# Attention and two MLPs on one core: product banks and sum banks of the second MLP as tiles of their own, weight sums moved to GpSimd, loads and stores issued a step later

## The chip, the cores and the metric

The kernel runs on one core of one Trainium2 chip. The metric is device time in microseconds (us) of one execution; shown are the median of three runs and one further execution that was profiled. Engines go by the profile's names: PE is the matrix engine, PEld its weight load, DVE, ACT and POOL are VectorE, ScalarE and GpSimd, and SP is the queue that issues all the DMAs spoken of here.

## The reference

```python
attn = softmax(q @ k.T / 8 + bias(pos))            # 4 batches, 8 heads, 576 positions, 64 wide
x = (attn @ v).transpose(0, 2, 1, 3).reshape(2304, 512)
h = x @ w_in                                       # 512 -> 2048
x = (h - tanh(h)) @ w_out                          # 2048 -> 512
g = sigmoid(x @ w_gate) * (x @ w_val)              # 512 -> 1536, twice
return g @ w_out2                                  # 1536 -> 512
```

Weights come as 64-bit floats in memory and are turned into pairs of 32-bit parts on the chip. A matrix product in full precision is three matmuls: high by high, high by low and low by high.

## The kernel before

**Three stages.** Attention fills the first 318 us or so, the first MLP runs to about 772 us, and the second MLP from there to the end. The first MLP goes in 48 steps (`n` in the loop at L943): `first(n)` is 24 matmuls of 128x384 at L639, `fifth(m)` 24 matmuls at L703, and between them ACT, DVE and POOL compute h - tanh(h) on the step before (L656 to L684). `x_load` (L623) fetches the tokens of a coming block (tile xm), which ACT then splits (L629) and POOL (L630).

**Weights of the second MLP** are converted alongside. A raw load (`load`, L500 and L504, tile wraw) is followed by an Abs on ACT (L521), four DVE operations (L548, L549, L550, L546), a cast on ACT (L584, high part) and a subtraction on POOL (L578, low part), then a store to a DRAM scratch (L582, tile wsc). For the seven-product scheme below, sums of the four quarters of a weight block are wanted too: items c0 and c1 of `make`, four DVE operations (L536, L537, L540, L541) for each of six weight groups fp. `run` hands out all of this, step by step; the last DVE operation of an item itself calls `load`, and the POOL operation itself issues the store. Four groups are converted during the first MLP, at n = 24, 30, 36 and 42; groups 4 and 5 are converted by `convert`, two operations or fewer to a slot, in the second MLP.

**Second MLP.** It is a row of 252 slots: 3 pairs of token blocks, 6 groups fp, and 14 products in each (7 for the gate with m = 0, then 7 for the value with m = 1; a seven-product scheme takes the place of eight block products). `slot2(s)` does `product(s)`: six matmuls of 128x384 at L829 into `banks[s % 2]`; then `down()`: three matmuls of 128x512 at L845 into one of six `sums`, for the group before; then `evacuate(s)`: one DVE or ACT operation that reads the bank (L873 to L890). In 12 of the 14 slots there is a `down()`; slots 12 and 13 of each group have none (called dry here, the others wet). `posts` runs what was put off: sigmoid, product of gate and value (POOL L901), split into gh (ACT L677) and gl (POOL L864).

Where products and sums live is decided at two places. Both banks are halves of one tile of the pool `up`, and two of the six sums are halves of another:

```python
b = up.tile([128, 2, 512], F32, name="up")
banks = [b[:, i, 0:TB] for i in range(2)]
...
b = up.tile([128, 2, 512], F32, name="up")
sums = [b[:, i] for i in range(2)]
```

Waits between engines are placed per tile by the tile framework: a write to one half of a tile counts as a write to the tile.

**Reloads.** `feed()` (L783, tile w from wsc) brings converted weights back, nine transfers of 512 KB for a group, through a ring of 13 slots, as soon as a slot's last reader has been given out (`spent`).

Of the kernel before, what the change touches and what calls it, by code (L numbers as in the profile page):

```python
# [7 lines left out]
F32 = mybir.dt.float32  # L8
# [5 lines left out]
PSUM = bass.MemoryType.PSUM  # L14
# [419 lines left out]
N1 = len(STEPS)  # L434
# [8 lines left out]
X0_AT = N1 - 4  # L443
# [10 lines left out]
class Weights:  # L454


    def __init__(self, nc, wi, wo, wg, wv, wo2, stage, wsc):
        self.nc, self.stage, self.wsc = nc, stage, wsc
        col = lambda w, n, f, k0, nk: dram_ap(w.bitcast(I32), 256 * f + 256 * n * k0, [[2 * n, 128], [256 * n, nk], [1, 256]])
        row = lambda w, f: dram_ap(w.bitcast(I32), 128 * f * 2 * DM, [[2 * DM, 128], [1, 2 * DM]])  # L460
        self.of = {}
        use = [("i", f) for f in range(FA)] + [("o", f) for f in range(FA)]
        for f in range(FA, NF1):
            use += [("i", f), ("o", f)]
        self.items = []
        for i, (k, f) in enumerate(use):
            self.of[k, f] = i
            self.items.append((k, f, [row(wo, f)] if k == "o" else [col(wi, DF1, f, 0, 4)]))
        for fp in range(NFP):
            for n in range(2):  # L470
                for k in range(2):
                    self.items.append((f"u{n}{k}", fp, [col(w, DF2, 2 * fp + n, 2 * k, 2) for w in (wg, wv)]))
            self.items += [("c0", fp, None), ("c1", fp, None)]
            self.items += [("p", 2 * fp + j, [row(wo2, 2 * fp + j)]) for j in range(2)]
        self.raws = [i for i, x in enumerate(self.items) if x[2]]
        self.n = len(self.items)
        self.raw, self.tmp, self.out, self.pools, self.u = {}, {}, {}, {}, {}
        self.loaded = self.scanned = self.made = self.done = self.usable = self.staged = 0
        self.stages = STAGE1
        self.turns = -1  # L480
        self.stored = set()

    def open(self, pool, lo, hi):
        self.limit = hi
# [41 lines left out]
    def make(self):  # L526
        i = self.made
        if i >= self.scanned:
            return []
        self.made += 1  # L530
        V = self.nc.vector
        k, f, src = self.items[i]
        if k == "c0":
            self.u["s"] = self.fresh(i)
            u = dict(self.u)
            return [lambda: V.tensor_add(u["s"], u["u10"], u["u11"]),  # L536
                    lambda: V.tensor_sub(u["u10"], u["u00"], u["u10"])]  # L537
        if k == "c1":
            u = dict(self.u)
            return [lambda: V.tensor_sub(u["u11"], u["s"], u["u00"]),  # L540
                    lambda: V.tensor_sub(u["u01"], u["u01"], u["u11"])]  # L541
        r, u = self.raw.pop(i), self.tmp[i]
        hi, lo, ui = r[:, :, 1], r[:, :, 0], u.bitcast(I32)

        def last():
            V.scalar_tensor_tensor(ui, lo, 29, ui, ALU.logical_shift_right, ALU.bitwise_or)  # L546
            self.load()
        return [lambda: V.tensor_scalar(u, u, HI_MIN, HI_MAX, ALU.max, ALU.min),  # L548
                lambda: V.tensor_scalar(ui, ui, 3, 0x3FFFFFF8, ALU.logical_shift_left, ALU.bitwise_and),  # L549
                lambda: V.scalar_tensor_tensor(ui, hi, -0x40000000, ui, ALU.bitwise_and, ALU.bitwise_or),  # L550
                last]

    def split(self):
        i = self.done
        if i >= self.made:
            return [], []
        self.done += 1
        k, f, src = self.items[i]
        if k in "io":
            parts = [(None, self.tmp.pop(i))]  # L560
        elif k == "p":
            parts = [((f // 2, GROUPS2 + f % 2), self.tmp.pop(i))]
        else:
            self.tmp.pop(i, None)
            u = self.u
            parts = {"u00": [(1, u.get("u00"))], "u01": [(2, u.get("u01"))], "u10": [], "u11": [(4, u.get("u11"))],
                     "c0": [(5, u.get("s")), (7, u.get("u10"))], "c1": [(6, u.get("u11")), (3, u.get("u01"))]}[k]
            parts = [((f, PRODUCTS.index(j)), x) for j, x in parts]
        highs, lows = [], []
        for at, x in parts:  # L570
            if at is None:
                w = self.out[i] = self.slot(i)
            else:
                w = self.slot(self.stages[self.staged % len(self.stages)])
                self.staged += 1

            def low(at=at, x=x, w=w):
                self.nc.gpsimd.tensor_sub(w[:, 1], x, w[:, 0].bitcast(F32))  # L578
                if at is None:
                    self.usable += 1  # L580
                else:
                    self.nc.sync.dma_start(self.wsc[at[0]][at[1]], w.bitcast(F32).rearrange("p a c -> p (a c)"))  # L582
                    self.stored.add(at)
            highs.append(lambda x=x, w=w: self.nc.scalar.copy(w[:, 0], x))  # L584
            lows.append(low)
        return highs, lows

    def trickle(self):
        while self.done < self.limit:
# [21 lines left out]
def mlps(tc, st, xr, x0, W, xs, x2s, out, consts):  # L611


    nc = tc.nc
    V, A, G, T = nc.vector, nc.scalar, nc.gpsimd, nc.tensor
    nq, nz, warm = consts
    TB = TBS[1]
# [120 lines left out]
    pk, ps, ob = (st.enter_context(tc.tile_pool(name=n, bufs=k)) for n, k in (("p2k", 2), ("p2s", 3), ("p2o", 4)))  # L738
    only1 = ExitStack()
    pm, pq = (only1.enter_context(tc.tile_pool(name=n, bufs=k)) for n, k in (("p2m", 2), ("p2q", 1)))  # L740
    up = st.enter_context(tc.tile_pool(name="ps_u", bufs=2, space=PSUM))

    TP = 2 * TB
    sx, xw, tt_ = {}, {}, {}
# [29 lines left out]
    ring, held, issued, spent = [], {}, [0], set()  # L774

    def feed():
        while issued[0] < len(loads):
            k = issued[0]
            tau, fp, i = loads[k]
            if (fp, i) not in W.stored or k >= len(ring) and (k < RING_SLOTS or loads[k - RING_SLOTS] not in spent):  # L780
                return
            w = W.slot(ring[k % RING_SLOTS])
            nc.sync.dma_start(w.bitcast(F32).rearrange("p a c -> p (a c)"), W.wsc[fp][i])  # L783
            held[loads[k]] = w
            issued[0] += 1
# [28 lines left out]
    def mat(s):  # L814
        g, j = divmod(s, GROUPS2)
        u, m = divmod(g, 2)
        tau, fp = divmod(u, NFP)
        return tau, fp, m, j

    def product(s):  # L820
        tau, fp, m, j = mat(s)
        w = held[tau, fp, j]
        p = banks[s % 2]
        fresh = j in (0, 1, 4)
        for kp in range(2):
            x = xw[PRODUCTS[j], kp]
            for i, (a, c) in enumerate(P3):
                o = 256 * m + 128 * kp
                T.matmul(p, w[:, a, o:o + 128], x[:, c], start=(fresh and kp == 0 and i == 0),  # L829
                         stop=(kp == 1 and i == 2), skip_group_check=True)  # L830
        if m:
            spent.add((tau, fp, j))
# [80 lines left out]

    def slot2(s):
        tau, fp, m, j = mat(s)
        product(s)
        left = down()
        evacuate(s)
        if left:
            at(s + 1, left)  # L920
        for f in posts.pop(s, []):
            f()
        if tau + 1 < NPAIR:
            if fp == 1 and m == 0 and j < 4:
                src_load(tau + 1, j)
            if fp == 2 and j < 3:
                combine(m, j)
            if fp == NFP - 1 and m == 1:
                x_next(j)
        feed()  # L930

    def x_next(j):
        k = PRODUCTS[j]
# [8 lines left out]
    temps = [0]  # L942
    s = 0  # L943
    for n in range(N1 + 3):
        if n == 2:
            acc = st.enter_context(tc.tile_pool(name="ps_a", bufs=4, space=PSUM))
        acts = second(n - 1) if ok(n - 1) else []
        acts[2:2] = [lambda m=m: fourth(m) for m in due(n, 1)]
        vecs = [f for m in due(n, 0) for f in third(m)]
# [27 lines left out]
        if ok(n):  # L977
            for _ in first(n):
                if n < 2:
                    yield  # L980
        elif n == N1:
            only1.close()
            ev = st.enter_context(tc.tile_pool(name="p3e", bufs=6))
            b = up.tile([128, 2, 512], F32, name="up")
            banks = [b[:, i, 0:TB] for i in range(2)]
            W.stages = RING[RING_SLOTS:]
            for _ in range(3):
                slot2(s)
                s += 1
        elif n == N1 + 1:  # L990
            b = up.tile([128, 2, 512], F32, name="up")
            sums = [b[:, i] for i in range(2)]
            for _ in range(4):
                slot2(s)
                s += 1
# [24 lines left out]
                    combine(kp, 3)  # L1020
                x_make(j, kp, V if j in (6, 7, 3) else G)
        if n >= X0_AT:
            ring += [i for i in RING if freed[i] == n + 1]
            ring[RING_SLOTS:] = []
            feed()
        yield
# [131 lines left out]
```

## Time and profile before

| what | value |
|---|---|
| median of three runs | 1308.53 us (1308.18 to 1310.28) |
| profiled execution, its time | 1310.77 us |
| its span, first to last instruction | 1309.0 us |
| mean granted clock of PE | 0.973 |
| PE busy | 1190.9 us, 91% of the span |
| DVE, ACT, POOL busy | 63%, 51%, 46% |

The profiled execution takes 2.24 us more than the median, and 1.77 us of its time lie outside its span. Busy shares are means over stages of different kinds. Matmuls are pipelined: the duration of one is longer than the distance from one to the next, so in a stretch without gaps PE's pace is read from how many matmuls it holds. A bracket behind a row of the timeline, as [0.65 <-DVE e L890], is idle time ahead of it and what ended that.

### The profile page before, as it was taken

The page shows a single profiled execution, that of the slowest core. Times are in us where ns is not written, and L with a number is a line of the kernel's source. Part 1 is how long each engine was busy: PE and PEld are TensorE (multiplying, and loading weights), DVE is VectorE, ACT ScalarE, POOL GpSimd, SP SyncE. Part 2 cuts the span into 40 slices and gives each one's busy share as a digit, 9 for nine tenths or more (in the row PEclk, how much of TensorE's full clock was granted, in tenths as well). Part 3 has the DMA queues.
Part 4 walks back from the last instruction along what each step waited for, and adds up shares of the span by engine and source line. Part 5 has one row for each costly group of instructions (what it writes and reads, how often), then busy time and mean ns, then how long its engine had stood idle before and what let it go on. Part 6 is the DMA issues. An engine that isn't in the chain of part 4 may idle for free.

```text
span 1309.0 us, 19878 instructions
## 1 busy us (share of the span) xinstructions
PE 1190.9 (91%) x6968; PEld 975.6 (75%) x6968; DVE 830.2 (63%) x1431; ACT 661.1 (51%) x1313; POOL 605.3 (46%) x558
## 2 busy tenths in 40 slices
PE   5789999999999999888977977888999999999998
PEld 2256676666899999788977976666777777777776
DVE  8978888885798888888879764764242322422222
ACT  7978788876566776655655542332141121321111
POOL 1067777775355555654546333544242322422322
PEclk9899999999999999898988979989999999999999
DMA  6656363632133334545464646867446554353551
GB/s 215 230 165 193 112 198 116 209 102 71 39 113 113 113 113 145 209 167 184 165 217 150 236 177 221 315 252 295 164 155 232 188 204 187 145 193 146 202 197 51
DMA packets 103027, 225.65 MB, mean 172 GB/s; under 512 B 12176, under 2 KB 52368, under 8 KB 102928
## 3 DMA queue, kind: packets, MB, share of 16 engines
q1 hardware_dynamic: 102928, 224.38, 48.9%
q8 instruction: 56, 0.92, 0.3%
q14 instruction: 43, 0.35, 0.1%
HBM read 166.26 MB, written 58.08 MB: 171 GB/s over the span
## 4 chain that ended last, share of the span: by engine, by line
PE 70%; DVE 11%; ACT 6%; DMA 5%; POOL 3%; issue 3%; SPq 0%; DVEq 0%; ACTq 0%; POOLq 0%
PE up L829 20%; PE acc L703 12%; PE up L639 12%; PE acc L845 6%; PE sc L227 5%; PE pv L319 5%; PE pt L269 5%; PE up L845 2%; DMA bsc<-e 1%; POOL gl L864 1%; DVE e L876 1%; DVE e L890 1%; PE bt L75 1%; DMA xm<-xs 1%; PE pv L316 1%
## 5 line engine op out<-in xcount | busy, mean ns | idle before, releaser
L829 PE MATMUL up<-w,w 128*128 128x384 f32 x1512 | 336.3, 358 | 45.1 <-DVE e L890 22.1
L829 PEld LDWEIGHTS up<-w,w 128*128 128x128 f32 x1512 | 255.3, 190 | 139.5 <-DVE e L890 46.5
L703 PE MATMUL acc<-gh,w 128*128 128x384 f32 x768 | 205.3, 349 | 32.7 <-DVE o L719 21.9
L639 PE MATMUL up<-xt,w 128*128 128x384 f32 x1152 | 210.1, 336 | 3.8 <-DVE t L673 3.8
L639 PEld LDWEIGHTS up<-xt,w 128*128 128x128 f32 x1152 | 201.6, 189 | 6.6 <-issue 6.6
L684 POOL TENSOR_TENSOR gl<-t,gh 128x384 fp32r<-128x384 f32 x96 | 106.7, 1129 | 147.2 <-ACT gh L677 55.7
L703 PEld LDWEIGHTS acc<-gh,w 128*128 128x128 f32 x768 | 145.9, 198 | 35.8 <-issue 22.8
L259 POOL TENSOR_SCALAR n<-n,rec 128x576 f32<-128x576 f32 x144 | 121.3, 857 | 81.6 <-DVE rec L254 42.7
L864 POOL TENSOR_TENSOR gl<-e,gh 128x384 fp32r<-128x384 f32 x54 | 56.8, 1053 | 220.3 <-ACT gh L677 219.1
L578 POOL TENSOR_TENSOR w<-wu,w 128x512 fp32r<-128x512 f32 x86 | 123.0, 1435 | 61.1 <-ACT w L584 60.8
L703 PE MATMUL acc<-gl,w 128*128 128x384 f32 x384 | 133.0, 346 | 0.0
L241 DVE CUSTOM_DVE_ANT_0 n<-sc,bias 128x576 f32<-128x576 f32 x144 | 103.7, 752 | 30.5 <-PE sc L227 22.8
L248 ACT ACTIVATE n<-n,mn 128x576 f32<-128x576 f32 x144 | 111.5, 784 | 8.0 <-DVE mn L241 7.7
L890 DVE TENSOR_TENSOR e<-up,e 128x384 f32<-128x384 f32 x72 | 40.2, 558 | 90.5 <-PE up L829 90.4
L677 ACT CAST gh<-t 128x384 fp32r<-128x384 f32 x114 | 57.1, 515 | 79.4 <-POOL t L901 59.5
L845 PE MATMUL acc<-w,gh 128*128 128x512 f32 x288 | 90.9, 396 | 0.0
L669 DVE TENSOR_TENSOR t<-up,t 128x768 f32<-128x768 f32 x48 | 45.9, 956 | 65.6 <-ACT t L656 65.6
L668 ACT ACTIVATE z<-z,c 128x768 f32<-128x768 f32 x48 | 45.1, 940 | 80.6 <-DVE up L667 80.6
L269 PE MATMUL pt<-ident,n 128*128 128x128 f32 x576 | 80.2, 280 | 1.4 <-ACT at L299 1.3
L630 POOL TENSOR_TENSOR xt<-xm,xt 128x384 fp32r<-128x384 f32 x48 | 50.3, 1069 | 65.6 <-ACT xt L629 60.6
L876 DVE TENSOR_TENSOR e<-up,e 128x384 f32<-128x384 f32 x36 | 20.0, 556 | 95.0 <-PE up L829 46.0
L319 PE MATMUL pv<-at,vs 128*64 128x320 f32 (+1 forms) x512 | 79.3, 421 | 0.0
(106 smaller groups left out, 2110.5 us busy)
## 6 DMA issues: line engine op xcount, KB each, us to landing
w<-wsc SPq DMA_DIRECT2D x162, 512.0 KB, 7.2
wsc<-w SPq DMA_DIRECT2D x54, 512.0 KB, 3.9
wraw<-in_wo SPq DMA_DIRECT2D x28, 512.0 KB, 4.0
bsc<-e SPq DMA_DIRECT2D x36, 295.5 KB, 3.2
xm<-xs SPq DMA_DIRECT2D x48, 192.0 KB, 3.8
x2s<-o SPq DMA_DIRECT2D x48, 192.0 KB, 3.3
wraw<-in_wi SPq DMA_DIRECT2D x16, 512.0 KB, 4.2
wraw<-in_wg SPq DMA_DIRECT2D x24, 256.0 KB, 2.9
```

Of the source, the lines that this page charges most:

```text
L241: V.tensor_tensor_reduce(n.rearrange("p (a b) -> p a b", a=2), s[:, :, 0:288], bias[t].rearrange("p (a b) -> p a b", a=2), -0.125, 3.0e38, ...
L248: A.activation(n, n, AF.Exp, bias=m, scale=-1.0, accum_out=nsum[u, t // 4][:, t % 4:t % 4 + 1])
L259: G.tensor_scalar(n, n, nrec[u, t // 4][:, t % 4:t % 4 + 1], 1.0, ALU.mult, ALU.mult)
L269: T.transpose(pt[:, i], n[:, o:o + 128], ident)
L319: T.matmul(p[0][64 * a:64 * a + 64, 0:N], v[:, c - 1, a], main[:, c - 1, a * N:a * N + N], start=False, stop=(c == 4))
L578: self.nc.gpsimd.tensor_sub(w[:, 1], x, w[:, 0].bitcast(F32))
L639: T.matmul(p[:, 0:TB], w[:, a, 128 * kt:128 * kt + 128], x[:, c], start=(kt == 0 and i == 0), stop=(kt == 3 and i == 2))
L684: G.tensor_sub(l, x[:, j], h.bitcast(F32))
L703: T.matmul(ac[blk][d][:, 0:TB], w[:, a, 128 * d:128 * d + 128], c, start=(begin and j == 0 and i == 0), stop=(end and j == NPR - 1 and i = ...
L829: T.matmul(p, w[:, a, o:o + 128], x[:, c], start=(fresh and kp == 0 and i == 0), stop=(kp == 1 and i == 2), skip_group_check=True)
L845: T.matmul(sums[3 * t + d], g[:, c], w[:, a], start=(begin and i == 0), stop=(end and i == 2))
L864: G.tensor_sub(l, x, h.bitcast(F32))
```

## The change

Five edits. (1) The two banks and two of the sums become four tiles `sum0` to `sum3` in a pool `ps_w`, opened where the pool `up` is closed; the pool `acc` of the other sums is put on the other side of the memory so that `up` can close. (2) The weight sums c0 and c1 run on GpSimd during the first MLP and on DVE again in the second. (3) Raw loads and stores of converted parts are no longer issued by the operation that frees or fills the buffer, but through a list `pending`, one step later in the first MLP and two slots later in the second. (4) `feed()` moves from the end of a slot to its start. (5) Ring slots are opened one step later.

```diff
+        self.mix = nc.gpsimd
+        self.clock = self.lag = 0
+        self.pending = []
+
+    def later(self, f):
+        if self.lag:
+            self.pending.append((self.clock + self.lag, f))
+        else:
+            f()
+
+    def tick(self):
+        self.clock += 1
+        while self.pending and self.pending[0][0] <= self.clock:
+            self.pending.pop(0)[1]()
...
-            return [lambda: V.tensor_add(u["s"], u["u10"], u["u11"]),
-                    lambda: V.tensor_sub(u["u10"], u["u00"], u["u10"])]
+            u, M = dict(self.u), self.mix
+            return [lambda: M.tensor_add(u["s"], u["u10"], u["u11"]),
+                    lambda: M.tensor_sub(u["u10"], u["u00"], u["u10"])]
...
-            self.load()
+            self.later(self.load)
...
-                    self.nc.sync.dma_start(self.wsc[at[0]][at[1]], w.bitcast(F32).rearrange("p a c -> p (a c)"))
-                    self.stored.add(at)
+                    self.later(lambda: self.store(at, w))
...
+    W.lag = 1
...
     def slot2(s):
         tau, fp, m, j = mat(s)
+        W.tick()
+        feed()
         product(s)
...
-        feed()
...
     for n in range(N1 + 3):
+        if n < N1:
+            W.tick()
         if n == 2:
-            acc = st.enter_context(tc.tile_pool(name="ps_a", bufs=4, space=PSUM))
+            acc = st.enter_context(tc.tile_pool(name="ps_a", bufs=4, space=PSUM, side="right"))
...
-            b = up.tile([128, 2, 512], F32, name="up")
-            banks = [b[:, i, 0:TB] for i in range(2)]
+            upst.close()
+            one = st.enter_context(tc.tile_pool(name="ps_w", bufs=1, space=PSUM))
+            four = [one.tile([128, 512], F32, name=f"sum{i}") for i in range(4)]
+            banks = [x[:, 0:TB] for x in four[:2]]
             W.stages = RING[RING_SLOTS:]
+            W.mix, W.lag = V, 2
...
-            b = up.tile([128, 2, 512], F32, name="up")
-            sums = [b[:, i] for i in range(2)]
+            sums = four[2:]
...
-            ring += [i for i in RING if freed[i] == n + 1]
+            ring += [i for i in RING if freed[i] == n or n == X0_AT and freed[i] < n]
```

The first place is PE's row in the second MLP, where one group of weights ends and the next begins. Before, both banks and a sum carry the name up; the number behind it tells the tile, and 9079 is the one tile of both banks.

```order
L829 MATMUL up_9079<-w10_8851,w30_10186 128x384 x3
L829 MATMUL up_9079<-w11_8962,w30_10186 128x384 x3
L829 MATMUL up_9079<-w12_8854,w25_10188 128x384 x3
L829 MATMUL up_9079<-w13_8965,w25_10188 128x384 x3
L829 MATMUL up_9079<-w0_10314,w20_10202 128x384 x3
L829 MATMUL up_9079<-w1_10317,w20_10202 128x384 x3
L845 MATMUL up_9146<-w16_10190,gh_10368 128x512 x2
L845 MATMUL up_9146<-w16_10190,gl_10369 128x512
```

Of the change, the same place:

```order
L848 MATMUL sum0_9075<-w10_8847,w30_10192 128x384 x3
L848 MATMUL sum0_9075<-w11_8958,w30_10192 128x384 x3
L848 MATMUL sum1_9076<-w12_8850,w25_10194 128x384 x3
L848 MATMUL sum1_9076<-w13_8961,w25_10194 128x384 x3
L848 MATMUL sum0_9075<-w0_10320,w20_10208 128x384 x3
L848 MATMUL sum0_9075<-w1_10323,w20_10208 128x384 x3
L864 MATMUL sum2_9077<-w16_10196,gh_10374 128x512 x2
L864 MATMUL sum2_9077<-w16_10196,gl_10375 128x512
```

No matmul has moved; products now go by turns to two tiles, and a product waits for the evacuation two slots back in place of that one slot back.

The second place is POOL's row in the first MLP, at the step of the first sums (n = 24). gl is the low part of h - tanh(h) that PE waits for, w the low part of a weight, wu a weight on its way. Before:

```order
L684 TENSOR_TENSOR gl_6777<-t_6694,gh_6776 128x384
L684 TENSOR_TENSOR gl_6781<-t_6694,gh_6780 128x384
L578 TENSOR_TENSOR w2_6772<-wu_6686,w2_6772 128x512
L578 TENSOR_TENSOR w3_6796<-wu_6773,w3_6796 128x512
L578 TENSOR_TENSOR w0_6797<-wu_6579,w0_6797 128x512
L578 TENSOR_TENSOR w1_6808<-wu_6686,w1_6808 128x512
L578 TENSOR_TENSOR w2_6809<-wu_6493,w2_6809 128x512
L684 TENSOR_TENSOR gl_6885<-t_6769,gh_6884 128x384
```

Of the change:

```order
L701 TENSOR_TENSOR gl_6777<-t_6694,gh_6776 128x384
L701 TENSOR_TENSOR gl_6781<-t_6694,gh_6780 128x384
L550 TENSOR_TENSOR wu_6773<-wu_6575,wu_6683 128x512
L551 TENSOR_TENSOR wu_6575<-wu_6409,wu_6575 128x512
L592 TENSOR_TENSOR w2_6772<-wu_6683,w2_6772 128x512
L554 TENSOR_TENSOR wu_6683<-wu_6773,wu_6409 128x512
L555 TENSOR_TENSOR wu_6490<-wu_6490,wu_6683 128x512
L592 TENSOR_TENSOR w3_6795<-wu_6773,w3_6795 128x512
L592 TENSOR_TENSOR w0_6796<-wu_6575,w0_6796 128x512
L592 TENSOR_TENSOR w1_6805<-wu_6683,w1_6805 128x512
L592 TENSOR_TENSOR w2_6806<-wu_6490,w2_6806 128x512
L701 TENSOR_TENSOR gl_6885<-t_6769,gh_6884 128x384
```

Four sums now stand on POOL between two steps' gl, where there were five subtractions; DVE's row is the same as before without them.

The third place is SP's row at the same step. xm is the load of tokens that the next steps need. Before:

```order
L723 DMA x2s<-o 128x384 x4
L582 DMA wsc_2_66<-w_6594 128x1024
L504 DMA wraw<-in_wo 128x1024
L582 DMA wsc_5_69<-w_6772 128x1024
L582 DMA wsc_4_68<-w_6796 128x1024
L582 DMA wsc_3_67<-w_6797 128x1024
L500 DMA wraw<-in_wg 128x2x256
L500 DMA wraw<-in_wv 128x2x256
L582 DMA wsc_1_65<-w_6808 128x1024
L582 DMA wsc_6_70<-w_6809 128x1024
L623 DMA xm<-xs 128x384 x2
```

Of the change:

```order
L740 DMA x2s<-o 128x384 x4
L518 DMA wraw<-in_wo 128x1024
L602 DMA wsc_2_66<-w_6594 128x1024
L518 DMA wraw<-in_wo 128x1024
L640 DMA xm<-xs 128x384 x2
L602 DMA wsc_5_69<-w_6772 128x1024
L602 DMA wsc_4_68<-w_6795 128x1024
L602 DMA wsc_3_67<-w_6796 128x1024
L514 DMA wraw<-in_wg 128x2x256
L514 DMA wraw<-in_wv 128x2x256
L602 DMA wsc_1_65<-w_6805 128x1024
L602 DMA wsc_6_70<-w_6806 128x1024
```

The pair of xm loads that stood behind five stores and two raw loads now stands ahead of them.

## Rows read from the trace of the kernel before

**Rows 1.** Page, the chain of work that ended last, by line.

```profile
PE up L829 20%; PE acc L703 12%; PE up L639 12%; PE acc L845 6%; PE sc L227 5%; PE pv L319 5%; PE pt L269 5%; PE up L845 2%; DMA bsc<-e 1%; POOL gl L864 1%; DVE e L876 1%; DVE e L890 1%; PE bt L75 1%; DMA xm<-xs 1%; PE pv L316 1%
```

**Rows 2.** Page, costliest groups of instructions, second MLP's products and evacuation.

```profile
L829 PE MATMUL up<-w,w 128*128 128x384 f32 x1512 | 336.3, 358 | 45.1 <-DVE e L890 22.1
...
L890 DVE TENSOR_TENSOR e<-up,e 128x384 f32<-128x384 f32 x72 | 40.2, 558 | 90.5 <-PE up L829 90.4
```

**Rows 3.** Timeline of PE, wet slots, then dry ones (start, us, engine, line).

```profile
1000.10 1.32 PE L829 MATMUL up<-w,w 128*128 128x384 f32 x6
1001.26 0.63 PE L845 MATMUL acc<-w,gh 128*128 128x512 f32 x2
1001.72 0.40 PE L845 MATMUL acc<-w,gl 128*128 128x512 f32 x1
1002.07 1.32 PE L829 MATMUL up<-w,w 128*128 128x384 f32 x6
...
1015.99 1.32 PE L829 MATMUL up<-w,w 128*128 128x384 f32 x6 [0.65 <-DVE e L890]
1017.96 0.45 PE L829 MATMUL up<-w,w 128*128 128x384 f32 x1 [0.65 <-DVE e L890]
```

**Rows 4.** Timeline of DVE in the first of those slots.

```profile
1001.46 0.56 DVE L890 TENSOR_TENSOR e<-up,e 128x384 f32<-128x384 f32 x1 [1.41 <-PE up L829]
```

**Rows 5.** Windows of the core, busy time of each engine, clock and DMA.

```profile
350.00:500.00 150.00, 150.00 (x864) 149.36 (x863) 134.43 (x174) 105.77 (x172) 82.02 (x71) 1.00 0.34 109
800.00:900.00 100.00, 84.06 (x376) 65.86 (x375) 63.51 (x96) 31.82 (x62) 49.88 (x40) 0.97 0.81 298
935.00:1296.00 361.00, 341.06 (x1556) 265.10 (x1555) 99.29 (x170) 81.42 (x166) 106.09 (x104) 1.00 0.46 177
```

**Rows 6.** Timeline of PE after the last product: sums back to back.

```profile
1296.86 0.62 PE L845 MATMUL up<-w,gh 128*128 128x512 f32 x2
...
1297.55 0.62 PE L845 MATMUL acc<-w,gh 128*128 128x512 f32 x2
```

**Rows 7.** Timeline: evacuations of slots 0, 70 and 251, the last.

```profile
777.32 0.48 ACT L873 COPY e<-up 128x384 f32<-128x384 f32 x1 [1.23 <-DVE t L673]
...
935.35 0.48 ACT L873 COPY e<-up 128x384 f32<-128x384 f32 x1 [3.80 <-PE up L829]
...
1296.35 0.56 DVE L890 TENSOR_TENSOR e<-up,e 128x384 f32<-128x384 f32 x1 [1.42 <-PE up L829]
```

**Rows 8.** Timeline, a stall in the first token pair.

```profile
852.42 0.66 ACT L521 ACTIVATE wu<-wraw 128x512 f32<-128x512 f32 x1 [4.46 <-DMA wraw<-in_wv]
...
854.52 0.69 PE L829 MATMUL up<-w,w 128*128 128x384 f32 x1 [4.48 <-DVE t L886]
```

**Rows 9.** DMA issues and SP's timeline: reloads (us to landing; then us issuing).

```profile
w<-wsc SPq DMA_DIRECT2D x162, 512.0 KB, 7.2
...
1014.07 4.95 SPq L783 DMA_DIRECT2D w<-wsc  x9
```

**Rows 10.** PE's waits from 490 to 775 us (total, times, longest).

```profile
PE acc L703 <- DVE o L719: 21.9, 3, 9.0
PE acc L703 <- ACT t L656: 5.1, 1, 5.1
PE acc L703 <- ACT o L722: 4.7, 1, 4.7
```

**Rows 11.** Timelines of SP and ACT, a late load of tokens.

```profile
535.14 2.21 SPq L623 DMA_DIRECT2D xm<-xs  x2
...
541.08 1.08 ACT L629 CAST xt<-xm 128x384 fp32r<-128x384 f32 x2 [3.08 <-DMA xm<-xs]
```

**Rows 12.** Timeline of DVE, weight sums (first, last of four); page, POOL's weight subtraction.

```profile
519.96 1.19 DVE L536 TENSOR_TENSOR wu<-wu 128x512 f32<-128x512 f32 x1
...
526.98 1.67 DVE L541 TENSOR_TENSOR wu<-wu 128x512 f32<-128x512 f32 x1
...
L578 POOL TENSOR_TENSOR w<-wu,w 128x512 fp32r<-128x512 f32 x86 | 123.0, 1435 | 61.1 <-ACT w L584 60.8
```

More of the change, by code (lines that the diff above doesn't have):

```diff
@@ L534, in make @@
             self.u["s"] = self.fresh(i)
-            u = dict(self.u)
-            return [lambda: V.tensor_add(u["s"], u["u10"], u["u11"]),
-                    lambda: V.tensor_sub(u["u10"], u["u00"], u["u10"])]
+            u, M = dict(self.u), self.mix
+            return [lambda: M.tensor_add(u["s"], u["u10"], u["u11"]),
+                    lambda: M.tensor_sub(u["u10"], u["u00"], u["u10"])]
         if k == "c1":
-            u = dict(self.u)
-            return [lambda: V.tensor_sub(u["u11"], u["s"], u["u00"]),
-                    lambda: V.tensor_sub(u["u01"], u["u01"], u["u11"])]
+            u, M = dict(self.u), self.mix
+            return [lambda: M.tensor_sub(u["u11"], u["s"], u["u00"]),
+                    lambda: M.tensor_sub(u["u01"], u["u01"], u["u11"])]
         r, u = self.raw.pop(i), self.tmp[i]
@@ L586, in split, with store @@
         return highs, lows
+    def store(self, at, w):
+        self.nc.sync.dma_start(self.wsc[at[0]][at[1]], w.bitcast(F32).rearrange("p a c -> p (a c)"))
+        self.stored.add(at)
     def trickle(self):
@@ L740, in mlps @@
     pm, pq = (only1.enter_context(tc.tile_pool(name=n, bufs=k)) for n, k in (("p2m", 2), ("p2q", 1)))
-    up = st.enter_context(tc.tile_pool(name="ps_u", bufs=2, space=PSUM))
+    upst = ExitStack()
+    up = upst.enter_context(tc.tile_pool(name="ps_u", bufs=2, space=PSUM))
+    W.lag = 1
     TP = 2 * TB
```

## The prediction

> **What bounds the kernel now.** I read the page's chain first. The largest line on it is the products of the second MLP, L829, with 20% of the span [rows 1]; PE is what the kernel waits for, and the question is at which pace it could go. The group of L829 tells of only 45.1 us of idle time before its matmuls, half of it put down to DVE's evacuation L890, while L890 in turn sat idle 90.4 us waiting for L829 [rows 2]. Two engines that wait for each other by turns are a ring: product, evacuation, product. The timeline shows it. A product starts at 1000.10, its six matmuls end at 1001.42, DVE reads the bank from 1001.46 to 1002.02, and the next product starts at 1002.07 [rows 3, 4]. A wet slot is so 1.97 us. A dry slot, which has three matmuls fewer, takes 1.97 us as well (1015.99 to 1017.96), with 0.65 us idle put down to L890 [rows 3]: the slot's length is that of the ring and not of PE's work. That the next product waits for the evacuation just before it, although it writes the other bank, is because both banks are one tile.
>
> PE's busy share hides this: from 935 to 1296 it is 341 of 361 us [rows 5], because the duration of a matmul overlaps that of the next. The pace without gaps is in the first MLP: 864 matmuls of 128x384 in 150.00 us at clock 1.00, with PE busy throughout [rows 5], 0.1736 us each. Six of them are 1.04 us. Three matmuls of 128x512 take 1297.55 - 1296.86 = 0.69 us when they follow each other [rows 6].
>
> **Own tiles for the banks (edit 1).** Without the ring a wet slot is 1.04 + 0.69 = 1.73 us and a dry one 1.04 us; a group of 14 slots is 14 x 1.04 + 12 x 0.69 = 22.9 us. I add 0.2 us a group for waits that are still there (semaphores, the copies out of the sums): 23.1 us, or 1.65 us a slot. Does the evacuation keep up? A product now waits for the evacuation two slots back. In a dry slot this is the tightest: the evacuation takes 0.56 us [rows 4], and from its end there is 0.05 us to the start of the next product; the product between takes 1.04 us, so the bank is free 0.4 us early. DVE, ACT and POOL are busy 99, 81 and 106 of 361 us [rows 5], so none of them is near a bound at 300 us.
>
> From the evacuation of slot 70 (935.35) to that of slot 251 (1296.35) are 361.0 us in 181 slots, 1.994 each [rows 7]. At 1.65 they take 298.7: **-62 us**. Bounds: with no added wait (22.9) -65; with 0.05 us more in every slot -53.
>
> The reloads must keep this pace. They come as a burst of nine per group, 4.95 us to issue at slot 12, landing a median 7.2 us after issue [rows 9]; the DMA engines are busy a share of 0.46 in that stretch [rows 5], which becomes 0.46 x 361 / 299 = 0.56. The median transfer lands 7.2 us after its issue, so the nine are in some 12 us (4.95 + 7.2) after the burst's start, and the group that reads them lasts 23. Closest are the first ones: by the ring's order they are read two dry and two wet slots after the start, 2 x 1.04 + 2 x 1.73 = 5.5 us at the new pace, 7.9 now. The early ones of a burst land before the median, so I cost this at nothing, and with it edit 4, which moves `feed()` from a slot's end to the next slot's start, the same instant for SP but for what that slot itself has spent. If the cover is gone, each of the 13 groups waits 1 to 2 us, 13 to 26 in all.
>
> **The first token pair, groups 0 to 4.** From 777.32 to 935.35 its 70 slots take 158.0 us [rows 7], 2.26 each; at the steady 1.994 they would take 139.6, so 18.4 us are stalls of other kinds. One is at 847 to 855: ACT's Abs waited 4.46 us for a raw load, DVE stood behind it, and PE waited 4.48 us for DVE's evacuation [rows 8]. If all these stalls stay, the gain is that of the ring alone, 70 x (1.994 - 1.65) = 24 us. I take 2 off for raw loads that are issued two slots later: **-22 us**. Bounds: -28, if the later issue and the freer banks take some of the stalls along; and -6, if from 800 to 900 nothing is gained, since DMA is busy 0.81 there [rows 5] and the same transfers in 0.83 of the time would be 0.98. Then only the other 58 us shrink, by a sixth, 10, less 4 for two slots more between a stage's release and its load.
>
> The start of the second MLP I cost at nothing: before, the second product waited for the ACT copy at 777.32, which itself stood behind the last DVE operation of the first MLP [rows 7]; after, the first product waits for that same operation, since the whole pool `up` is closed.
>
> **Sums on POOL (edit 2).** Sixteen DVE operations of 1.19 to 1.67 us [rows 12] go to POOL, where a subtraction of the same shape takes 1.435 us [rows 12], four of them 5.7 us against about 5 on DVE. They are not queued ahead of something that was early: before, POOL sat idle 60.8 us waiting for the casts of ACT [rows 12], and those casts stood behind the sums. The next step's gl is behind them on POOL, now as before. I take 0 to 1 us for each step: -2 in all. The three waits for L719, 21.9 us [rows 10], I leave as they are: that operation follows the conversion on DVE, whose two-input operations run beside POOL's subtractions just the same.
>
> **Loads and stores a step later (edit 3).** Here SP's order counts. Before, the xm pair was issued at 535.14, behind five stores that wait for POOL, and ACT then stood 3.08 us for it at 541.08 [rows 11]. PE's waits of 4.7 and 5.1 us in this stretch [rows 10] follow on two such late loads, each on an ACT operation behind the cast. With xm ahead of the stores both should go: 9.8 us, of which I take 8. The raw loads come one step, 8.3 us, later; they had been loaded ahead into a few buffers, so that cover may be thin. With the sums that makes **-10 us** for the first MLP; bounds -16 (part of the L719 waits goes along) and +3 (the later raw loads are missed in some steps).
>
> Edit 5 shifts the first reloads by one step at 771, before the second MLP begins; nothing.
>
> **Sum.** 62 + 22 + 10 = 94 us. The profiled execution took 1310.8 us and ran 2.2 us over the median: 1310.8 - 94 - 2 = **1215 us**.
>
> A rule of the Trainium skill speaks against edit 1. The page TensorE: Matmul & The Clock Gate, section "HAM oscillation — how this bites in real kernels", reports of a kernel whose loop had already been rearranged: "Adding PSUM double-buffering gave no further gain". The row shows a dry slot with 0.65 us of idle put down to the evacuation [rows 3]; by the rule the sum would lack the 62 us and most of the 22, by the row it has them. I go by the row, and keep the rule as a rival.
>
> **Rivals.** *A: the first pair becomes bound by conversion and DMA.* For it: the share of 0.81 and the wait for a raw load [rows 5, 8]. Against: outside the stalls its slots run at the ring's 1.97. Then the first pair gives 6 in place of 22: 1231 us. *B: POOL's sums lengthen the steps in which they run.* For it: nine POOL operations of 1.435 us, 12.9 us, now stand between two steps' gl where a step is 8.3 us (48 x 0.1736). Against: the idle time named above. If the four sums are all on PE's path, 4 x 5.7 = 23 us: 1238 us. By the page GPSIMD Engine Reference, section 4.1, an elementwise operation with two inputs should not go to GpSimd, being about twice as slow as on VectorE; this is the same rival. *C: the pitch of slots hardly falls,* because the product then waits for something with the same period. This is what the rule on double-buffering would give. For it: nothing in the timeline, which shows nothing else between evacuation and product. Then only some 20 us of 94 are left, 1290 us; the edit doing nothing at all, 1308, is part of this case. *D, the other side: PE's clock falls once it has no gaps.* A group is 22.9 us at clock 1.00 and 22.9/c at c; it is as long as the 27.8 us now (14 x 1.99) at c = 0.82. At 0.75 it is 30.5, 13 groups lose 35 us, and with 32 from elsewhere used up the kernel is slower by a few us, 1312. Against: in the stretch without gaps the clock was 1.00 for 150 us, and it fell only where PE waited, 0.97 at 800 to 900 [rows 5].
>
> **How the numbers follow.** The forecast has 0.66, A 0.16, B 0.08, the loss of reload slack (1228 to 1241) 0.03, C 0.04, D 0.03. The likeliest gives 1215. Its own bounds are 1310.8 - 2.2 - (65 + 28 + 16) = 1200 and, with 53, 12 and 4, 1240; with A and B as they stand the range is 1196 to 1243, and what is left out is C, D, and A and B together. A measurement here tells 0.2% (2.6 us) from nothing. Faster by more: all but D and part of C, 0.95; same 0.02; slower 0.03.
>
> **What would show it.** In the timeline at 950 to 1250 products 1.73 us apart, 1.04 in dry slots, and no wait of L829 for DVE; groups of 23 us; clock 1.00 there. ACT's 3.08 us for xm gone, the waits for L719 still at some 22 us. In the first pair the stalls for raw loads at their present size. The prediction is wrong if dry slots stay near 2 us (C), if DMA share passes 0.95 with longer waits of ACT for wraw (A), if POOL is named ahead of PE's waits at the steps with sums (B), or if the granted clock leaves 1.00 in a stretch without gaps (D).

## The result and the profile after

The changed kernel takes 1229.33 us (median of four runs, 1225.06 to 1230.97) against 1309.4 us before on the same chip: a ratio of 0.9378, with a 95% interval of 0.9344 to 0.9413. Its profiled execution has a span of 1229.2 us, 79.8 us less than the 1309.0 of before.

PE's timeline in the middle of the second MLP, which answers to [rows 3]; L848 are the products now, L864 the sums:

```profile
953.33 0.63 PE L864 MATMUL acc<-w,gh 128*128 128x512 f32 x2
953.79 0.40 PE L864 MATMUL acc<-w,gl 128*128 128x512 f32 x1
954.03 1.22 PE L848 MATMUL sum<-w,w 128*128 128x384 f32 x6
...
955.79 1.22 PE L848 MATMUL sum<-w,w 128*128 128x384 f32 x6
...
959.31 3.30 PE L848 MATMUL sum<-w,w 128*128 128x384 f32 x18
962.45 0.63 PE L864 MATMUL sum<-w,gh 128*128 128x512 f32 x2
```

A wet slot is 1.76 us from one product to the next (954.03 to 955.79), and the two dry slots run into the next group's first product: 18 matmuls in one row, with no idle time named ahead of any, 3.14 us for three products (959.31 to 962.45), 1.05 each. The windows say the same of the whole stretch (compare the last row of [rows 5]; engines' busy time, then clock, DMA share and GB/s):

```profile
800.00:900.00 100.00, 82.89 (x386) 74.79 (x385) 59.52 (x90) 30.24 (x59) 52.70 (x42) 0.88 0.79 297
916.00:1216.00 300.00, 299.98 (x1549) 277.91 (x1548) 99.58 (x169) 80.17 (x165) 106.39 (x104) 1.00 0.57 215
```

PE is busy 299.98 of 300 us at a granted clock of 1.00, DMA 0.57 of the time. The upper row is another matter: in the first token pair the clock is 0.88, where it was 0.97 [rows 5].

The evacuations of slots 0, 70 and 251 stand here, as in [rows 7]:

```profile
772.10 0.48 ACT L892 COPY e<-sum 128x384 f32<-128x384 f32 x1 [3.53 <-PE sum L848]
...
915.94 0.48 ACT L892 COPY e<-sum 128x384 f32<-128x384 f32 x1 [1.70 <-PE sum L848]
...
1217.16 0.56 DVE L909 TENSOR_TENSOR e<-sum,e 128x384 f32<-128x384 f32 x1 [0.48 <-PE sum L848]
```

Groups 0 to 4 take 143.8 us (158.0 before), groups 5 to 17 301.2 us (361.0 before). I read the same marks, and ACT's squares of the first and last step of the first MLP, from the timeline of every run; the table holds these three stages. They are a sharper measure than the medians, since the first step's square, with only the attention ahead of it, moves between 322 and 327 us by itself from one profiled execution to the next. They come from one execution of each kernel, and runs that share the code of a stage tell how far it moves by itself: the first MLP took 443.3 and 445.8 us (e1, before), 438.9 to 440.3 (changed, e2, e4, e5, e7) and 424.6 to 427.2 (e6, e9, e11); groups 0 to 4 took 142.1 to 143.8 (changed, e3, e6, e12). A difference of 2 us in a stage says little. Each ratio is to the kernel before, run beside it on the same chip. Line numbers of one statement differ by some lines from kernel to kernel.

| run | first MLP | groups 0 to 4 | groups 5 to 17 | median, us | ratio to before (95%) |
|---|---|---|---|---|---|
| before | 445.8 | 158.0 | 361.0 | 1309.4 | |
| changed | 439.0 | 143.8 | 301.2 | 1229.3 | 0.9378 (0.9344 to 0.9413) |
| e1 banks alone | 443.3 | 138.5 | 301.3 | 1232.0 | 0.9407 (0.9391 to 0.9424) |
| e2 all but banks | 439.0 | 158.8 | 360.6 | 1304.2 | 0.9962 (0.9952 to 0.9973) |
| e3 sums on DVE | 435.5 | 143.8 | 301.3 | 1228.6 | 0.9380 (0.9362 to 0.9398) |
| e4 no lag, second MLP | 439.4 | 141.6 | 301.3 | 1228.2 | 0.9380 (0.9356 to 0.9404) |
| e5 reloads spread | 440.3 | 132.7 | 301.8 | 1219.9 | 0.9319 (0.9304 to 0.9334) |
| e6 block sums early | 426.9 | 142.1 | 301.2 | 1215.1 | 0.9262 (0.9244 to 0.9280) |
| e7 no conversion | 438.9 | 117.4 | 301.2 | 1209.2, one run | |
| e8 parts undone | 436.0 | 140.3 | 301.2 | 1226.1 | 0.9357 (0.9344 to 0.9370) |
| e9 e5 and e6 | 424.6 | 131.4 | 301.8 | 1206.1 | 0.9222 (0.9197 to 0.9247) |
| e10 e9, sums on DVE | 429.0 | 132.9 | 302.2 | 1210.8 | 0.9251 (0.9233 to 0.9269) |
| e11 e9, later Abs | 427.2 | 131.2 | 301.6 | 1206.4 | 0.9219 (0.9201 to 0.9236) |
| e12 no lag, first MLP | 442.9 | 143.6 | 301.3 | 1235.5 | 0.9424 (0.9402 to 0.9445) |

### The profile page after: what moved, and what is told of

It is laid out like the page before. It is cut to its first block, busy times and chain, and to the rows that moved or that the text cites. A ratio compares the mean times of both kernels' runs of the same rounds, so it can differ in the third digit from the quotient of the medians.

```text
span 1229.2 us, 19862 instructions
## 1 busy us (share of the span) xinstructions
PE 1137.2 (93%) x6968; PEld 993.5 (81%) x6968; DVE 814.2 (66%) x1415; ACT 660.2 (54%) x1313; POOL 622.5 (51%) x574
## 4 chain that ended last, share of the span: by engine, by line
PE 73%; DVE 7%; DMA 6%; issue 5%; POOL 5%; ACT 4%; SPq 0%; DVEq 0%; ACTq 0%; POOLq 0%
PE sum L848 19%; PE acc L720 13%; PE up L656 11%; PE acc L864 7%; PE sc L227 6%; PE pv L319 5%; PE pt L269 5%; PE sum L864 3%; DMA wsc<-w 2%; DMA bsc<-e 2%; POOL w L592 2%; PE bt L75 1%; DMA wraw<-in_wv 1%; PE pv L316 1%; ACT z L673 1%
## 5 line engine op out<-in xcount | busy, mean ns | idle before, releaser
L848 PE MATMUL sum<-w,w 128*128 128x384 f32 x1512 | 309.0, 344 | 22.7 <-DVE t L905 12.1
L848 PEld LDWEIGHTS sum<-w,w 128*128 128x128 f32 x1512 | 276.7, 192 | 46.6 <-DVE t L905 13.4
L720 PE MATMUL acc<-gh,w 128*128 128x384 f32 x768 | 203.5, 347 | 27.0 <-DVE o L736 21.1
L701 POOL TENSOR_TENSOR gl<-t,gh 128x384 fp32r<-128x384 f32 x96 | 103.0, 1093 | 127.2 <-issue 57.3
L864 PE MATMUL acc<-w,gh 128*128 128x512 f32 x288 | 91.4, 398 | 0.0
L909 DVE TENSOR_TENSOR e<-sum,e 128x384 f32<-128x384 f32 x72 | 40.0, 556 | 60.3 <-PE sum L848 60.2
L562 DVE TENSOR_SCALAR wu<-wu 128x512 f32<-128x512 f32 x68 | 54.3, 799 | 38.6 <-ACT wu L535 38.5
L720 PEld LDWEIGHTS acc<-gl,w 128*128 128x128 f32 x384 | 75.1, 196 | 3.3 <-POOL gl L701 3.3
```

Of the source, the lines that this page charges most:

```text
L701: G.tensor_sub(l, x[:, j], h.bitcast(F32))
L720: T.matmul(ac[blk][d][:, 0:TB], w[:, a, 128 * d:128 * d + 128], c, start=(begin and j == 0 and i == 0), stop=(end and j == NPR - 1 and i = ...
L864: T.matmul(sums[3 * t + d], g[:, c], w[:, a], start=(begin and i == 0), stop=(end and i == 2))
```

## The experiments

**The banks alone, and all but the banks (e1, e2).** e1 puts only these lines into the kernel before; e2 takes only them out of the changed one.

```diff
-            banks = [b[:, i, 0:TB] for i in range(2)]
+            four = [one.tile([128, 512], F32, name=f"sum{i}") for i in range(4)]
+            banks = [x[:, 0:TB] for x in four[:2]]
...
-            sums = [b[:, i] for i in range(2)]
+            sums = four[2:]
```

> The kernel before with edit 1 alone (own tiles for banks and sums). Theory T, the ring of product and evacuation is nearly the whole gain: groups 5 to 17 fall from 361 to about 301 us as in the changed kernel, the first MLP stays as before (last ACT square at 770 us), and the first token pair gains at least the 14 us of the changed kernel, since the later loads and stores (edit 3) are not there to cost anything: 1309 - 60 - 14 to 24 = 1225 to 1235 us. Rival R, the pace in the second MLP also needs the moved feed and the later stores: groups of clearly more than 23.2 us and a time of 1245 us or more.

> The changed kernel with edit 1 undone (banks and sums again halves of two tiles), edits 2 to 5 kept. Theory T: the slots are 1.97 us again, groups 6 to 17 are 27.8 us, and only the 5 to 8 us of the first MLP are left: 1300 to 1305 us. If the other edits carry more than that, the time is under 1295 us; if they cost (later raw loads in the first pair), it is 1308 us or more.

With edit 1 alone groups 5 to 17 take 301.3 us, without it 360.6: the steady pace of the second MLP is edit 1 and nothing else, and rival R falls. In e2 dry slots wait for the evacuation as before:

```profile
1007.48 1.31 PE L847 MATMUL up<-w,w 128*128 128x384 f32 x6 [0.65 <-DVE e L908]
```

Edits 2 to 5 without edit 1 give a ratio of 0.9962, some 5 us, all of it in the first MLP (439.0 against the 443.3 and 445.8 of e1 and before). In the first pair they cost: 138.5 us with the banks alone, 143.8 with everything.

**Weight sums back on DVE (e3)**, in the changed kernel:

```diff
-        self.mix = nc.gpsimd
+        self.mix = nc.vector
```

> The changed kernel with the weight sums of the first MLP back on DVE, all else as changed. Theory: their place is off PE's path, since the casts of ACT follow the sums on either engine; the time is that of the changed kernel within 3 us (1226 to 1232), and the two long waits of PE for the block sums (L736) stay at 8 us each. Rival B of the prediction: POOL's sums lengthen their steps; then this kernel is 5 to 20 us faster, 1210 to 1224 us. Third: they relieve DVE, and this kernel is 3 to 8 us slower.

The medians do not tell the two apart. By stage, the first MLP is 435.5 in place of 439.0 us: beside the lag of edit 3 the sums on POOL cost 3.5 us (2.9 to 4.8 with e8, which has the same first MLP as e3, and the five runs that share that of the changed kernel). PE's long waits for the block sums stay where the sums are on DVE (6.7 us at most, 8.0 on POOL).

**No lag in the second MLP (e4)**:

```diff
-            W.mix, W.lag = V, 2
+            W.mix, W.lag = V, 0
```

> The changed kernel with raw loads and part stores of the second MLP issued at once again (lag 0 in place of 2), the first MLP as changed. Theory L: the first token pair fell short of its forecast (143.8 us for groups 0 to 4, forecast 136) because raw loads are issued two slots late and then land behind a burst of reloads, so ACT waited 7.2 and 9.1 us for them; without the lag these waits fall below 4 us and the pair gains 6 to 12 us: 1217 to 1223 us. Rival A of the prediction: the DMA engines are full there whenever the loads are issued; the waits keep their sum and the time stays within 1226 to 1232 us. Third: the loads issued at once block SP's queue ahead of the reloads, and PE waits for reloads: slower, over 1233 us.

Theory L falls. The first pair gains 2.2 us, not 6 to 12, hardly more than this stage moves by itself, and the median is the same. ACT's waits for raw loads there are 15.3 us in place of 20.4. The rows that settle it are those of e1, where loads were issued at once too (ACT's waits in groups 0 to 4; total, times, longest):

```profile
ACT wu L521 <- DMA wraw<-in_wv: 16.0, 3, 9.1
ACT wu L521 <- DMA wraw<-in_wo: 2.9, 1, 2.9
```

In the kernel before these two are 4.7 and 2.2 us, and in e2, with the slow slots and the late issue, 6.3 and 1.7. It is the faster slots that uncover the raw loads, not the moment of their issue.

**Reloads spread (e5)**, where `feed(most)` issues at most so many reloads:

```diff
-        feed()
+        feed(1)
```

> The changed kernel with at most one reload issued per slot of the second MLP, in place of bursts of seven to nine. Theory A2, raw loads land late because they queue in the DMA engines behind a burst of reloads (a load issued at 836.7 landed at 841.7, when the 12 reloads issued from 825 on were in): with reloads spread, ACT's waits for raw loads, 20.4 us in 797 to 876, fall below 8 us and groups 0 to 4 fall from 143.8 to 130 to 138 us, 1216 to 1224 us in all. Rival: the raw loads are late only because of when they are issued; the waits stay near 20 us and the time within 1226 to 1232 us. Third: single reloads come too late for their product; PE waits for DMA and groups 5 to 17 are longer than 23.2 us.

The time came as theory A2 forecast, 132.7 us and 1219.9, but not by the row that it named: ACT still waited 17.0 us for raw loads, in six pieces of which the longest is 7.3. What fell is what reached PE. Its waits in groups 0 to 4, of the changed kernel and of e5:

```profile
PE sum L848 <- DVE t L905: 12.1, 3, 7.1
PE sum L848 <- ACT e L892: 3.7, 1, 3.7
```

```profile
PE sum L849 <- DVE t L906: 5.0, 4, 1.8
PE sum L849 <- DVE e L902: 2.7, 2, 2.3
```

So the burst matters, and the sum of ACT's waits does not measure it. The expectation misnames its example: the load of 836.74 landed at 845.57, and what ACT took at 841.69 had been issued at 831.61, behind eight reloads (its rows stand in the next section). That is theory A2's queue, with a longer wait in it than was read: 10.0 us. The median from issue to landing of the raw loads at L514 in groups 0 to 4 is 7.9 us in the changed kernel and 6.7 in e5.

**Block sums early (e6)**, at the two steps with weight sums and a block's end:

```diff
             W.scan()
+            if scans == 2:
+                for m in due(n - 1, 2):
+                    if ends(m):
+                        sixth(m)
         run()
...
-            if ends(m):
+            if ends(m) and scans < 3:
```

> The changed kernel with the block sums (L736) put ahead of the four conversion operations on DVE in the two steps that have both weight sums and the end of a block (n = 30 and 42); nothing else moves. Theory: PE's two waits of 8.0 us for L736 come from DVE's order, since DVE stood behind an Abs that waited for POOL's sums; both fall under 2 us, and stretch 29 to 34 of the first MLP (53.8 us) and 41 to 47 (69.0 us) lose 6 to 10 us each: 1209 to 1219 us. Rival: the block sums themselves, or the stores of weights behind them on SP, bound these steps; the waits move to another line and under 4 us are won in all.

The stretch from step 29 to 34 falls from 53.8 to 46.8 us, that from 41 to 47 from 69.0 to 64.2, the second short of the 6 us expected: 12 us in all, the median 14. The changed kernel shows why, on DVE and then on ACT and PE:

```profile
581.73 0.90 DVE L562 TENSOR_SCALAR wu<-wu 128x512 f32<-128x512 f32 x1 [3.38 <-ACT wu L535]
...
587.29 1.94 DVE L736 TENSOR_TENSOR o<-acc,o 128x384 f32<-128x384 f32 x4
```

```profile
581.03 0.67 ACT L535 ACTIVATE wu<-wraw 128x512 f32<-128x512 f32 x1 [1.98 <-POOL wu L554]
```

```profile
587.98 0.98 PE L720 MATMUL acc<-gh,w 128*128 128x384 f32 x2 [7.96 <-DVE o L736]
```

L736 needs nothing of the conversion; it stood behind four operations that waited for ACT, which waited for a sum on POOL. In e6 the two long waits for L736 are gone; the one that is left comes near the end of the first MLP, where the changed kernel has it too (3.55 us at 750.26), and POOL's gl is now the longest in total of PE's waits in 490 to 765:

```profile
PE acc L720 <- POOL gl L701: 9.4, 5, 3.8
...
PE acc L720 <- DVE o L736: 3.5, 1, 3.5
```

**No conversion in the second MLP (e7)**:

```diff
+    stop = [x[:2] for x in W.items].index(("u00", 4))
...
-        while W.done < W.n:
+        while W.done < stop:
...
-            nc.sync.dma_start(w.bitcast(F32).rearrange("p a c -> p (a c)"), W.wsc[fp][i])
+            nc.sync.dma_start(w.bitcast(F32).rearrange("p a c -> p (a c)"), W.wsc[fp % 4][i])
```

> The changed kernel without the conversion of weight groups 4 and 5 in the second MLP (they are read from the scratch of groups 0 and 1; the output is not the reference's). It prices the conversion and its raw loads. Theory A (conversion and its transfers are all that holds up the first pair): groups 1 to 4 run at 23 to 24 us each, group 0 keeps the two blocks of 24 matmuls that belong to the first MLP (26 us), 120 us in all in place of 143.8, about 1205 us. Rival: reloads alone are late in the first pair, since the ring's slots come free late there; then groups 1 to 3 stay above 26 us.

Groups 1 to 4 run at 23.2 to 23.3 us and the pair takes 117.4: the conversion of two weight groups, with its raw loads and stores, costs 26 us of the changed kernel's 143.8, and the reloads alone cost nothing (PE waits 0.3 us in all there).

**Three parts undone (e8)**: the edits of e3 and e4, and `feed()` at the end of `slot2` again.

> The changed kernel with the three parts undone that seem to cost: weight sums of the first MLP on DVE, no lag in the second MLP, feed at a slot's end; edit 1 and the lag of the first MLP stay. If the prices of single runs add up: the first MLP 435.5 us (439.0 as changed), groups 0 to 4 138.5 us as with edit 1 alone (143.8 as changed): 1219 to 1223 us. If the place of feed does nothing, groups 0 to 4 stay at 141.6 and the time is 1223 to 1226 us. If undoing them only frees what something else then takes, 1226 us or more.

Its median is 1226.1, at the edge of the third answer. The first MLP has its gain (436.0), the first pair (140.3) stands between e4 and e1. The last 2 us between e8 and e1 are about what this stage moves by itself.

**Both together (e9), with sums on DVE (e10), with a later Abs (e11).** e11 adds one `yield` ahead of `W.scan()` in `convert`.

> The changed kernel with the early block sums and the spread reloads together. If the two stalls are apart (one in the first MLP, one in the first token pair) the gains add: first MLP 427 us, groups 0 to 4 133 us, 1229 - 12 - 11 = 1204 to 1208 us. If they share something (conversion that comes earlier meets the burst elsewhere), 1209 us or more.

> As the run with both, and the weight sums of the first MLP on DVE. With the early block sums PE waited 9.4 us for gl of POOL in 490 to 765 (2.3 us in the changed kernel), since four sums and five subtractions stand ahead of gl. If POOL's sums are now what is left of the stalls at n = 30 and 42, this kernel gains 4 to 9 us over the run with both; if the sums are off the path on either engine, it is the same within 3 us; if DVE then delays the block sums again, it loses 3 us or more.

> As the run with both, and in the second MLP the Abs of each weight item stands one slot later in ACT's order, so that a raw load has 1.7 us more before ACT stands still for it. Theory: what is left of the first pair's stall (17 us of ACT's waits in six pieces, 132.7 us for groups 0 to 4 against 117.4 without conversion) is ACT standing ahead of PE's evacuations; the waits lose 1.7 us each and groups 0 to 4 fall to 123 to 130 us, 4 to 9 us faster than the run with both. Rival: the raw loads are bound by DMA's throughput, conversion only ends later, and the reloads of groups 4 and 5 come late: same or slower.

The gains of e5 and e6 add: e9 takes 1206.1 us, level with e11 at the head of all, and by the ratios 1.7% under the changed kernel. e10 is the third answer of its expectation: 429.0 us in the first MLP, 2 to 4 us more than in the three runs with the sums on POOL and early block sums. PE's waits for L736 in 490 to 765 are 14.7 us there and 8.8 in e9, those for gl are gone (7.9 in e9); the sums on DVE stand ahead of the block sums, and with these moved early POOL is the better place. e11 did to the row what was wanted and won nothing, as its rival has it. ACT's wait for raw loads fell from 16.3 to 5.3 us, and a wait of PE for reloads took its place, which was 0.3 us in e9 (group 4 takes 27.3 us, 23.6 in e9):

```profile
ACT wu L535 <- DMA wraw<-in_wv: 5.3, 2, 4.0
```

```profile
PE sum L851 <- DMA w<-wsc: 5.9, 4, 2.4
```

**No lag in the first MLP (e12)**:

```diff
-    W.lag = 1
+    W.lag = 0
```

> The changed kernel with loads and stores of the first MLP issued at once again (lag 0 in place of 1), the second MLP as changed. Theory: the whole gain in the first MLP comes from xm loads that stand ahead of stores in SP's row; without the lag ACT waits some 3 us for xm near 541 again, PE's two waits of 4.7 and 5.1 us behind it are back, and the first MLP goes from 439.0 to 445 to 450 us: 1235 to 1241 us. Rival: the gain comes from the stores and raw loads themselves being out of the way; then ACT's wait for xm stays small and the first MLP still grows, with PE's waits on other lines. Third: the lag does nothing, 1226 to 1232 us.

The waits that edit 3 was to remove are back, on ACT and on PE:

```profile
ACT xt L646 <- DMA xm<-xs: 5.6, 2, 2.8
```

```profile
PE acc L720 <- ACT t L673: 6.7, 1, 6.7
PE acc L720 <- ACT o L739: 4.3, 1, 4.3
```

They come to 11.0 us, where the changed kernel still waits 4.9 at the same two places (1.3 and 3.6), but the first MLP is only 3.9 us longer (442.9, short of the 445 expected): from step 29 to 34 e12 is 2.5 us shorter than the changed kernel. The lag gives and takes, and it matters where the sums are. With the sums on DVE the lag is worth 7.3 to 10.3 us (443.3 and 445.8 in e1 and before, 435.5 and 436.0 in e3 and e8), with the sums on POOL 2.6 to 4.0. Read the other way, the sums on POOL cost some 3 to 5 us beside the lag and gain 0.4 to 2.9 without it.

## Why the prediction was right, point by point

The forecast was 1215 us in a range of 1196 to 1243; it came to 1229. The direction, the mechanism and the largest term were right, and about 14 of the 94 us did not come.

**Own tiles, -62 forecast, -59.8 measured.** A group is 23.2 us (23.1 forecast). The ring was the only thing between 27.8 and PE's own pace. The rule of the Trainium skill that spoke against it (page TensorE: Matmul & The Clock Gate, section "HAM oscillation — how this bites in real kernels") is a report on one kernel and does not carry over to this one: here edit 1 alone gives 0.9407, and rival C falls. Rival D falls too: PE ran 300 us without a gap at clock 1.00.

**First pair, -22 forecast, -14.2 measured.** This term was mis-sized, and it is the step "if all these stalls stay" that failed: the stalls were taken as fixed, and only the ring's part as shrinking. They are waits for transfers whose number does not shrink with the slots. ACT's waits for raw loads in groups 0 to 4 were 6.9 us before, 18.9 with edit 1 alone, 20.4 as changed. The gain lies in group 0 (36.7 us before, 26.1 after) and group 4 (27.8 and 23.3); groups 1 to 3, where ACT waits, took 93.6 us before and 94.5 after, so that there nothing was gained, as rival A has it for 800 to 900. The price is 8 of the 16 us given there, and the reason is not quite rival A's: over 800 to 900 the DMA share is 0.79, not 0.98, and e5 runs the same transfers 11 us faster. The engines are full in a burst: 0.97 from 825 to 842. The 2 us for the lag came out at 2.2 (e4), hardly more than this stage moves by itself; for the 5.3 us between the changed kernel and e1 see the last section. One such wait in the changed kernel, on SP, the time in us from issue to landing of the second of these issues, the DMA share (the last number but one) from the burst to the landing, then ACT and PE:

```profile
825.42 4.55 SPq L802 DMA_DIRECT2D w<-wsc  x8
...
831.61 0.38 SPq L514 DMA_DIRECT2D wraw<-in_wv  x1
```

```profile
wraw<-in_wv SPq DMA_DIRECT2D x1, 256.0 KB, 10.0
```

```profile
825.00:842.00 17.00, 11.50 (x59) 10.08 (x57) 10.36 (x13) 3.19 (x7) 9.24 (x7) 0.91 0.97 355
```

```profile
841.69 0.66 ACT L535 ACTIVATE wu<-wraw 128x512 f32<-128x512 f32 x1 [9.13 <-DMA wraw<-in_wv]
```

```profile
843.79 2.29 PE L848 MATMUL sum<-w,w 128*128 128x384 f32 x6 [7.07 <-DVE t L905]
```

The load lands at 841.61, 10.0 us after its issue, behind the eight reloads: each of the 85 transfers that SP issued in groups 0 to 4 landed after the one issued before it. The issue itself stands two slots behind the operation that freed the buffer. ACT has stood 9.13 us, DVE's evacuation behind it, PE 7.07, and then PE's six matmuls take 2.29 us where they take 1.22.

**First MLP, -10 forecast, -6.8 measured.** The 445.8 us of before can be 443.3 by themselves (e1), so the gain is 3 to 7 us. ACT's xm waits went as forecast; of PE's two waits behind them, 9.8 us, 4.9 are left. With the sums on DVE (e3) the gain is 8 to 10 us, as much as was forecast for the two edits together. Two things took some of it. The sums on POOL, forecast at -2, cost 3.5 beside the lag (e3): rival B, at a sixth of its price. One sum there takes 1.26 to 1.30 us, so four of them 5.1 and not 5.7, and POOL is named ahead of PE for 2.3 us in all. And stores that are issued a step later hold the buffers of the converted parts longer: ACT, which waited for no such store before, now does in two places:

```profile
ACT w L597 <- DMA wsc<-w: 21.7, 2, 11.2
```

In e6, with the same lag, these two waits are 3.5 us together: one step later the stores stand in SP's row behind those of L736's results (issued at 587.87, the weights' at 589.73), so that most of this wait is L736's lateness, passed on by the lag. PE sees little of it (step 29 to 34 is 0.6 us longer than before), as the waits for L736 stand beside it. Those stayed as forecast: 21.1 us, 21.9 before [rows 10].

**The start and the rest.** The second MLP's first product came later and its third slot sooner: from the last step's square to the evacuation of slot 2 are 12.3 us, 12.7 before; nothing, as forecast. But slot 0's evacuation, the mark where groups 0 to 4 begin, comes 9.1 us after that square and came 6.8 before, which lends the first pair 2.3 of its 14.2 us. The reloads' cover held (no product waits for them after 916).

**The shortfall of 14 us** is then 2.2 in the steady groups, 7.8 in the first pair, 3.2 in the first MLP, and 1 in the attention, the start and the end taken together.

**The range.** Its upper end is not what the terms say: the sum for 1240 takes 53, 12 and 4, while the bounds written beside the terms are 53, 6 and a loss of 3, which give 1253. Nor is it said how 1200 and 1240 become 1196 and 1243. The 1229 measured lies inside either way.

## What to carry to other kernels

Two engines that wait for each other by turns, with idle time on both, are a ring; before a buffer is doubled for it, look whether two buffers are there already and one tile holds both. When a ring goes, the waits that were hidden beside it do not keep their size: here those for raw loads went from 6.9 to 18.9 us by the faster slots alone. So cost such a stretch by what stands in the queue ahead of each load, and not by its old stalls. The prices of two edits need not add: the sums on POOL gained without the lag and cost beside it. And look for an operation that stands in an engine's row behind work that it doesn't need; moving L736 by four places was worth more here than edits 2 to 5 together.

## What the runs showed of the hardware

A long wait of PE can cost twice. In the first pair the granted clock was 0.96 before, 0.91 in the changed kernel with waits up to 7.1 us, and 0.99 in e9, as the windows of groups 0 to 4 of the changed kernel and of e9 show:

```profile
772.00:916.00 144.00, 126.23 (x615) 116.11 (x614) 78.22 (x121) 40.65 (x81) 65.70 (x53) 0.91 0.69 256
```

```profile
757.00:889.00 132.00, 120.92 (x617) 109.86 (x616) 83.31 (x121) 41.28 (x81) 66.22 (x53) 0.99 0.77 279
```

Both rows hold the same work of PE, 615 and 617 matmul records. In the changed kernel the clock fell to the lower of its two levels (0.50) within the three longest of PE's waits there, of 4.53, 7.07 and 3.71 us, and PE began again at that level:

```profile
810.83:815.20 4.37, 4.37 (x13) 4.09 (x14) 2.99 (x5) 1.67 (x3) 0.65 (x2) 0.50 0.61 238
843.79:849.30 5.51, 5.51 (x16) 5.22 (x17) 3.38 (x5) 2.03 (x4) 3.31 (x3) 0.50 0.66 232
881.61:886.80 5.19, 5.19 (x15) 4.90 (x16) 3.29 (x5) 1.96 (x4) 3.40 (x4) 0.50 0.64 255
```

In all, PE worked 17.3 us at 0.50 in groups 0 to 4 of the changed kernel, 11.8 in e1 and 2.7 in e9, and it waited 17.6, 15.2 and 11.0 us there. If half of the work at half the clock is loss, waits and clock come to 26, 21 and 12 us. This is an estimate from these numbers; by it the changed kernel loses 5 us against e1 and 14 against e9, where the groups differ by 5.3 and 12.4.

The DMA engines carry the same transfers at a share of 0.69 and 0.77: 99 and 102 us of work. That is less than the 117.4 us that the pair takes without conversion (e7), so that over the whole pair the DMA engines are not the bound, though in a burst they are full. Another buffer for raw loads, which might take the last of the stalls, was not tried.
